# A linear attention with a ReGLU FFN on one core: the first batch in smaller pieces, wo in three loads, the second batch's x turned by DMA, and a new order

## Chip, core and metric

One NeuronCore of a Trainium2 chip runs the whole kernel. The metric is the device time of one execution in microseconds (us); lower is better. The engines are TensorE (PE; its weight loads are shown as PEld), VectorE (DVE), ScalarE (ACT), GpSimd (POOL) and SyncE (SP). SP, ACT and POOL also issue DMA transfers, each from a queue of its own, in the order in which its instructions stand.

## What is computed

```python
# q, k, v: (8 batches, 8 heads, 576 tokens, 64), w_phi: (64, 128)
def phi(x):
    proj = np.einsum('bhsd,df->bhsf', x, w_phi)
    proj = proj - np.max(np.abs(proj), axis=-1, keepdims=True)
    return np.concatenate([np.exp(proj), np.exp(-proj)], axis=-1)
q_p, k_p = phi(q), phi(k)
kv = np.einsum('bhsf,bhsd->bhfd', k_p, v)
z = np.sum(k_p, axis=2)
num = np.einsum('bhsf,bhfd->bhsd', q_p, kv)
den = np.einsum('bhsf,bhf->bhs', q_p, z)[..., None] + 1e-06
x = (num / den).transpose(0, 2, 1, 3).reshape(4608, 512)
# the FFN: w_gate and w_val (512, 1536), w_out (1536, 512)
out = (np.maximum(x @ w_gate, 0) * (x @ w_val)) @ w_out   # float32
```

## The kernel before

**Tiling.** The first 512 tokens of a batch are its main part, 4 chunks of 128; the last 64 are its tail, and the tails of two batches make one chunk of 128. The matmuls are in bf16 and add up in PSUM in f32; a `bank` is one of PSUM's 8 banks (128 partitions by 512 f32).

**Attention.** For k, the 64 x 128 projection is multiplied with the turned k (kT; matmuls L312, "rows"), DVE takes the largest absolute value of each token and head (L319), ACT takes both exponents of the projection (L368, kp) and those of the maximum (L379, ek), and POOL multiplies v with ek (L328, vs) and appends the ek themselves (L414). The kv matmuls (L509 for batches 0 and 1, L486 for the others) add kp against vs over the tokens, and ACT or DVE copies the result to SBUF (L422). For q, the same projection is made twice: as columns (L549), from which ACT takes the exponents qp (L567) without a maximum, and as rows (L312) for the maximum (L319), whose exponent is cq (L583). The n matmuls (L597) multiply qp with kv in three groups of heads; DVE joins their two halves, t = second half times cq (L616) and u = first half plus t (L628), takes the reciprocal of the denominator (L635), and POOL or DVE makes x (L642, xu).

**Turning.** The matmuls need k, q and x with their features on the partitions. `TURN = 2`: for batches 0 and 1 k, q and x are turned by TensorE with an identity matrix (L271, four 128 x 128 blocks a bank for x) and copied from PSUM by DVE or ACT (L284, for x L662). From batch 2 on the DMA crossbar turns them, issued by SP (L292 for k and q, L298 for the tails, L650 for x, one issue per chunk).

**FFN.** Group g = 0 to 7 holds the main tokens of batch g, group 8 the tails. For each block of 128 of the 1536 hidden features, four matmuls make val and four gate (L734), ACT or DVE copies val to SBUF (L749), and DVE makes h = max(gate, 0) times val (L756). Then 12 matmuls with wo per chunk (L791, in three atoms of four), a copy (L805) and the store (L772, for the tails L776 on two queues). `FIRST` says in which pieces of tokens and blocks group 0 goes: it starts when two of its four chunks of x are turned. `LAST` splits the output columns of the last chunk into 352 and 160.

**Loads.** q, k and the weights (wv and wg in thirds, L243; wo, L252) are loaded by POOL's queue, which casts them to bf16; v by SP's queue in f32 (L214, L220). The tails go by L236.

**The order.** All this is cut into "atoms", each a function that issues a few instructions. `ORDER`, a string of numbers, says in which order the atoms are issued; a `'` picks the other engine where there are two, and `z3` issues three matmuls on zeros that only keep TensorE busy (L200). As every engine and queue works in its own order, the string sets what each does next. The sequence of the groups is that of a pipeline: while the FFN of one batch runs on TensorE, the attention of the next batches stands between its matmuls.

## Time and profile before

| | |
|---|---|
| time, median of 3 runs (lowest to highest) | 379.01 us (378.92 to 380.15) |
| profiled execution: span from first to last instruction | 377.4 us |
| difference between the median and this span | 1.6 us |
| mean granted TensorE clock in the profiled execution | 0.995 |
| TensorE busy in the span | 368.1 us |

The profile shows one execution. Busy times count an engine's instructions; "issue ... landing" is the time from a DMA's issue to the arrival of its data; rows of the timeline give the start, the duration, the engine, the line and the tiles, with neighbouring instructions of one kind joined (x4), and in brackets the idle time before them with what ended it. The duration of a joined row of matmuls contains the tail of the last one in the pipeline, so the next row starts before its end.

### The profile page before, as it was taken

The numbers are of one execution on the slowest core, as the hardware profiler recorded it, in microseconds if no ns is written. First come the engines' busy times: TensorE is split into PE (matmuls) and PEld (weight loads), VectorE is DVE, ScalarE is ACT, GpSimd is POOL, SyncE is SP. The second block draws the span as 40 slices with busy tenths as digits, with TensorE's granted clock in tenths as the row PEclk, the third lists the DMA queues.
The fourth block names the chain that finished last, engine by engine and source line by source line (L and its number), as shares of the span: only waits on it lengthen the run. The fifth ranks groups of instructions, "written<-read, shape, count | busy, mean of one in ns | idle before, by whom it ended". The sixth has DMA issues, their size and how long they took to land.

```text
span 377.4 us, 8960 instructions
## 1 busy us (share of the span) xinstructions
PE 368.1 (98%) x3502; PEld 197.4 (52%) x3502; DVE 290.7 (77%) x633; ACT 213.1 (56%) x509; POOL 151.3 (40%) x201
## 2 busy tenths in 40 slices
PE   7789999999999999999999999999999999999996
PEld 4568465546545555464554554465455444444443
DVE  6998999988876799888868886988768927824641
ACT  6997888877687556876765359882740302111101
POOL 5883672488275275901842126933700210000000
PEclk9899999999999999999999999999999999999999
DMA  8999999999489959781289678620410130021004
GB/s 260 205 200 215 233 131 174 219 172 137 89 213 236 165 67 171 144 182 28 59 160 179 96 174 132 130 16 16 128 41 2 29 113 29 2 67 58 2 2 109
DMA packets 87929, 45.10 MB, mean 120 GB/s; under 512 B 55824, under 2 KB 82000, under 8 KB 87888
## 3 DMA queue, kind: packets, MB, share of 16 engines
q1 hardware_dynamic: 60208, 30.42, 37.3%
q0 software_dynamic: 27200, 13.57, 28.8%
q8 instruction: 27, 0.44, 0.5%
q10 hardware_dynamic: 480, 0.56, 0.5%
q14 instruction: 14, 0.11, 0.1%
HBM read 37.78 MB, written 9.44 MB: 125 GB/s over the span
## 4 chain that ended last, share of the span: by engine, by line
PE 92%; ACT 3%; DMA 3%; issue 0%; SPq 0%; DVE 0%; POOL 0%; DVEq 0%
PE pa L734 49%; PE pa L791 25%; PE pa L597 5%; PE pa L312 5%; PE pa L486 4%; PE pa L549 2%; DMA qn<-in_q_dram 2%; ACT qp L567 2%; PE pa L271 1%; PE pa L509 1%; DMA vn<-in_k_dram 1%; ACT kp L368 1%; ACT kv L422 0%; ACT val_sb L749 0%; ACT xT L662 0%
## 5 line engine op out<-in xcount | busy, mean ns | idle before, releaser
L791 PE MATMUL pa<-wo_sb,h 128*128 128x512 bf16 (+2 forms) x444 | 99.9, 373 | 0.0
L734 PE MATMUL pa<-xT,wv_sb 128*128 128x512 bf16 (+1 forms) x400 | 99.3, 370 | 0.1
L734 PE MATMUL pa<-xT,wg_sb 128*128 128x512 bf16 (+1 forms) x400 | 99.3, 370 | 0.0
L756 DVE SCALAR_TENSOR_TENSOR h<-pa,val_sb 128x512 bf16<-128x512 f32 (+1 forms) x112 | 74.6, 669 | 27.2 <-PE pa L734 20.5
L749 ACT CAST val_sb<-pa 128x512 bf16<-128x512 f32 (+1 forms) x67 | 38.1, 575 | 97.1 <-PE pa L734 88.0
L567 ACT ACTIVATE qp<-pa 128x512 bf16<-128x512 f32 x144 | 76.2, 618 | 15.1 <-PE pa L549 14.8
L368 ACT ACTIVATE kp<-pa 128x512 bf16<-128x512 f32 (+1 forms) x152 | 77.4, 605 | 11.1 <-PE pa L312 9.8
L328 POOL TENSOR_TENSOR vs<-vn,ek 128x512 bf16<-128x512 f32 (+1 forms) x68 | 67.4, 1005 | 31.1 <-DMA vn<-in_v_dram 15.2
L734 PEld LDWEIGHTS <-wv_sb 128*128 128x128 bf16 x448 | 41.9, 98 | 44.9 <-issue 1.2
L734 PEld LDWEIGHTS <-wg_sb 128*128 128x128 bf16 x448 | 41.6, 98 | 43.5 <-issue 0.7
L791 PEld LDWEIGHTS <-h 128*128 128x128 bf16 x444 | 40.8, 98 | 44.6 <-issue 0.8
L319 DVE TENSOR_REDUCE mq<-pa 128x4 f32<-128x512 f32 x72 | 46.5, 683 | 10.4 <-PE pa L312 10.1
L319 DVE TENSOR_REDUCE mk<-pa 128x4 f32<-128x512 f32 (+1 forms) x76 | 47.8, 653 | 3.9 <-ACT kp L368 2.3
L642 POOL TENSOR_TENSOR xu<-u,r 128x512 bf16<-128x512 f32 x22 | 22.8, 1041 | 67.4 <-DVE r L635 53.5
L642 POOL TENSOR_TENSOR tT<-u,r 128x512 bf16<-128x512 f32 x14 | 14.6, 1042 | 73.0 <-DVE r L635 41.0
L628 DVE TENSOR_TENSOR u<-pa,t 128x195 f32<-128x195 f32 (+3 forms) x120 | 38.2, 333 | 3.3
L616 DVE TENSOR_TENSOR t<-pa,cq 128x195 f32<-128x195 f32 (+3 forms) x120 | 36.8, 325 | 2.2 <-PE pa L597 1.0
L597 PEld LDWEIGHTS <-qp 128*128 128x128 bf16 x640 | 28.1, 98 | 14.0 <-ACT qp L567 0.9
L749 DVE CAST val_sb<-pa 128x512 bf16<-128x512 f32 (+1 forms) x45 | 30.7, 682 | 4.5 <-PE pa L734 3.0
L597 PE MATMUL pa<-kv,qp 128*128 128x65 bf16 x640 | 31.0, 193 | 0.9 <-ACT qp L567 0.5
L805 DVE COPY out_sb<-pa 128x512 f32<-128x512 f32 x13 | 8.9, 688 | 13.8 <-PE pa L791 13.6
L486 PEld LDWEIGHTS <-kp 128*128 128x128 bf16 x480 | 16.6, 98 | 3.9 <-issue 0.7
(71 smaller groups left out, 278.4 us busy)
## 6 DMA issues: line engine op xcount, KB each, us to landing
vn<-in_v_dram SPq DMA_DIRECT2D x6, 1024.0 KB, 7.3
qn<-in_q_dram POOLq DMA_DIRECT2D x8, 512.0 KB, 8.6
out_dram<-tT SPq DMA_DIRECT2D x16, 256.0 KB, 2.9
out_dram<-out_sb SPq DMA_DIRECT2D x16, 256.0 KB, 2.9
kn<-in_k_dram POOLq DMA_DIRECT2D x6, 512.0 KB, 9.1
wv_sb<-in_moe_w_val_dram POOLq DMA_DIRECT2D x3, 512.0 KB, 10.2
wg_sb<-in_moe_w_gate_dram POOLq DMA_DIRECT2D x3, 512.0 KB, 9.1
wo_sb<-in_moe_w_out_dram POOLq DMA_DIRECT2D x1, 1536.0 KB, 19.5
```

Of the source, the lines that this page charges most:

```text
L319: nc.vector.tensor_reduce(m, some.rearrange("p (c f) -> p c f", f=F), axis=AX.X, op=ALU.max, apply_absolute_value=True,)
L328: eng.tensor_tensor(dst[:, :, s, 0:D], src, ek[:, :, s : s + 1].to_broadcast(list(src.shape)), op=ALU.mult,)
L368: nc.scalar.activation(st["kp"][:, s, 0 : n // 2, par, :], st["banks"][par][:, 0 : n // 2 * F].rearrange("p (a f) -> p a f", f=F), AF.Exp, ...
L567: nc.scalar.activation(x["qp"][:, s, slot].rearrange("p a b -> p (a b)"), st["cols", i][par], AF.Exp, scale=sign,)
L597: nc.tensor.matmul(pn[:, E * (2 * i + s) : E * (2 * i + s + 1)], lhsT=x["qp"][:, s, slot, blk, :], rhs=kv_of(b, lo + i)[:, s, :],)
L616: nc.vector.tensor_tensor(x["t", j][rows, 0:n], ab[:, :, 1], c[:, :, None].to_broadcast([np_, n, E]), op=ALU.mult,)
L628: nc.vector.tensor_tensor(x["u"][rows, lo : lo + n], ab[:, :, 0], x["t", j][rows, 0:n], op=ALU.add)
L642: copy_of(alt, nc.gpsimd, nc.vector).tensor_tensor(x["xu"], x["u"][:, :, 0:D], x["r"].to_broadcast([P, H, D]), op=ALU.mult)
L734: nc.tensor.matmul(ps, lhsT=w[:, dc, P * fi : P * fi + P], rhs=xTs[g][:, dc, lo:hi], start=(dc == 0), stop=(dc == NDC - 1),)
L749: copy_by(copy_of(alt, "ACT", "DVE"))(st["val", n], ps)
L756: nc.vector.scalar_tensor_tensor(st["h2"][:, fi, lo:hi], ps, 0.0, st["val", n], op0=ALU.max, op1=ALU.mult)
L791: nc.tensor.matmul(po, lhsT=st["h2"][:, fi, P * t : P * t + P], rhs=wo_sb[:, fi, c0:c1], start=(fi == 0), stop=(fi == NFC - 1),)
```

## The change

- `FIRST` has five pieces: blocks 0 to 3 with chunk 0 alone, then with chunk 1, blocks 4 to 7 with chunks 0 and 1, blocks 0 to 7 with chunks 2 and 3, blocks 8 to 11 with all. A bank now holds as many blocks side by side as fill 512 columns (four, two or one), so val's copy and h's product always have 512 columns. Group 0 has 12 steps instead of 16.
- `SPLIT`: the column and row matmuls of batch 0's q are issued one bank at a time, and cq is made for each chunk apart.
- `KV_LAST`: the kv matmuls of batch 0 are issued in two parts, the last four blocks of tokens in the second.
- `X_TURN = 1`: x of batch 1 is turned by the DMA crossbar, issued by SP; k and q of batch 1 are still turned on TensorE.
- wo is loaded in three parts of four blocks each.
- The buffer of an xu and of an output tile is chosen by the chunk's number, not by a running count.
- `ORDER` is new. It issues 5 matmuls on zeros instead of 6. (`PLAIN` is empty, so what hangs on it does nothing.)

```diff
+Q_TURN = 2
+X_TURN = 1
-FIRST = ((0, 2, 0, 4), (2, 4, 0, 4), (0, 4, 4, 12))
+FIRST = ((0, 1, 0, 4), (1, 2, 0, 4), (0, 2, 4, 8), (2, 4, 0, 8), (0, 4, 8, 12))
...
-ORDER = """7 z3 82 92 93 83' 84 87 94 86 8 0 98 102 85 89 90 91 88 103 z1 104 96 97 108 105 95 107 106 z1 112
...
+PLAIN = set()
+SPLIT = {(0, 0), (0, 1)}
+KV_LAST = {0: 4}
+ORDER = """z3 84 94 85 86 87 104 95 96 88 89 105 z1 106 114 90 99 9 10 98 97 124 107 109 115 91 116 0 125 134
...
+    def load_wo(i):
+        part = slice(4 * i, 4 * (i + 1))
+        nc.gpsimd.dma_start(
+            out=wo_sb[:, part], in_=moe_w_out.rearrange("(c p) n -> p c n", p=P)[:, part]
         )
+    for i in range(NFC // 4):
+        atoms.add("ld", f"wo{i}")(lambda alt, i=i: load_wo(i))
...
+        last = [x for x in order if x[2] >= 2 * CP * (part + 1) - KV_LAST.get(b, 0)]
+        order = [x for x in order if x not in last] + last
+        cuts = [0, len(order) - len(last), len(order)]
+        for piece, (lo, hi) in enumerate(zip(cuts, cuts[1:])):
...
+            for pars in ((0,), (1,)) if split else ((0, 1),):
+                at = (i, *pars) if split else (i,)
+                @atoms.add("qc", *key, *at)
+                def _(alt, i=i, pars=pars):
+                    for par in pars:
+                        st["cols", i, par] = bank()
...
-            b >= TURN,
-            blocks if b < TURN else None,
+            b >= X_TURN,
+            blocks if b < Q_TURN else None,
...
-        steps = [(fi, 0, SF) for fi in range(NFC)]
+        steps = [(fi, 1, 0, SF) for fi in range(NFC)]
         if g == 0:
-            steps = [(fi, P * lo, P * hi) for lo, hi, f0, f1 in FIRST for fi in range(f0, f1)]
+            steps = [
+                (fi, C // (hi - lo), P * lo, P * hi)
+                for lo, hi, f0, f1 in FIRST
+                for fi in range(f0, f1, C // (hi - lo))
+            ]
+        def half_step(fi, nf, w, lo, hi):
+            ps = bank().rearrange("p (f n) -> p f n", f=nf)
+            for i in range(nf):
+                for dc in range(NDC):
+                    nc.tensor.matmul(
+                        ps[:, i],
+                        lhsT=w[:, dc, P * (fi + i) : P * (fi + i + 1)],
+                        rhs=xTs[g][:, dc, lo:hi],
```

Three places of the new order. First POOL, near the start: here batch 0's v is multiplied (vs), and the loads of wg, wv and of batch 1's q are issued. Before:

```order
L328 TENSOR_TENSOR vs<-vn_109,ek 128x8x64
L414 CAST vs<-ek 128x16
L243 DMA wg_sb<-in_moe_w_gate_dram 128x4x512
L328 TENSOR_TENSOR vs<-vn_109,ek 128x8x64 x2
L414 CAST vs<-ek 128x16
L214 DMA qn<-in_q_dram 128x8x256
L243 DMA wv_sb<-in_moe_w_val_dram 128x4x512
```

And of the change:

```order
L230 DMA qn<-in_q_dram 128x8x256
L349 TENSOR_TENSOR vs<-vn_109,ek 128x8x64 x2
L468 CAST vs<-ek 128x16
L349 TENSOR_TENSOR vs<-vn_109,ek 128x4x64
L468 CAST vs<-ek 128x8
L349 TENSOR_TENSOR vs<-vn_109,ek 128x4x64
L259 DMA wg_sb<-in_moe_w_gate_dram 128x4x512
L259 DMA wv_sb<-in_moe_w_val_dram 128x4x512
```

The load of wg's first third stood between two vs of batch 0 and ahead of batch 1's q; now it stands behind the last vs of batch 0 and behind that q.

Second SP, where batches 1 and 2 meet: qT0 is the turn of batch 2's q, kmT that of the k tails, vn0 the load of batch 2's v, xT_1543 the turned x of batch 1. Before:

```order
L298 DMA_TRANSPOSE kmT_1283<-km_1280 128x4x128
L292 DMA_TRANSPOSE qT0_1390<-qn_1388 128x16x128
L772 DMA out_0_dram<-tT8_1484 128x512
L772 DMA out_0_dram<-out_sb_1596 128x512
L292 DMA_TRANSPOSE kT1_1607<-kn_1503 128x16x128
L214 DMA vn0_1635<-in_v_dram 128x8x256
```

And of the change:

```order
L319 DMA_TRANSPOSE kmT_1508<-km_898 128x4x128
L719 DMA_TRANSPOSE xT_1543<-tT4_1538 128x4x128
L848 DMA out_0_dram<-tT8_1566 128x512
L313 DMA_TRANSPOSE qT0_1634<-qn_1524 128x16x128
L719 DMA_TRANSPOSE xT_1543<-xu_1651 128x4x128
L719 DMA_TRANSPOSE xT_1543<-xu_1672 128x4x128
L719 DMA_TRANSPOSE xT_1543<-tT4_1644 128x4x128
L848 DMA out_0_dram<-tT8_1708 128x512
L230 DMA vn0_1752<-in_v_dram 128x8x256
```

Four turns of x are new on this queue, three of them between the turn of batch 2's q and the load of its v.

Third DVE, its last instructions of the program (tT and out_sb are output tiles, u the buffer of the second piece of the last chunk). Before:

```order
L756 SCALAR_TENSOR_TENSOR h_6191<-pa,val_sb 128x512
L805 COPY tT_6354<-pa 128x512
L805 COPY tT_6388<-pa 128x512
L805 COPY u<-pa 128x160
```

And of the change:

```order
L830 SCALAR_TENSOR_TENSOR h_6237<-pa,val_sb 128x512 x3
L881 COPY tT_6404<-pa 128x512
L881 COPY tT_6412<-pa 128x512
L881 COPY out_sb<-pa 128x512
L881 COPY out_sb<-pa 128x352
```

The piece of 160 columns is copied earlier and by ACT now; the piece of 352 columns comes last and is copied by DVE.

More of the change, by code (lines that the diff above doesn't have):

```diff
@@ L284, in turned_copy @@
         copy_by(by)(st["T"].rearrange("p a b -> p (a b)"), st["pt"][:, 0 : n * P])
-    for b in range(TURN, B):
-        for n in "kq":
+    for b in range(min(TURN, Q_TURN), B):
+        for n, first in (("k", TURN), ("q", Q_TURN)):
+            if b < first:
+                continue
             @atoms.add("turn", n, b)
@@ L310, in rows_of @@
         for j in range(T.shape[1]):
-            for par in range(2):
+            for par in banks:
                 nc.tensor.matmul(
@@ L351, in _ @@
                 st["T"] = T()
-            st["banks"] = [bank(), bank()]
+            st["banks"] = {par: bank() for par in range(2)}
             rows_of(st["T"], st["banks"])
@@ L373, in _ @@
                     )
+        if plain:
+            return
         @atoms.add("kk", *key)
@@ L751, in _ @@
+        for n, (fi, nf, lo, hi) in enumerate(steps):
+            @atoms.add("fv", g, n)
+            def _(alt, n=n, fi=fi, nf=nf, lo=lo, hi=hi):
+                ps = half_step(fi, nf, wv_sb, lo, hi)
+                st["val", n] = sb_g.tile([P, SF], BF16, name="val_sb")
+                copy_by(copy_of(alt, "ACT", "DVE"))(
+                    st["val", n], ps.rearrange("p f n -> p (f n)")
+                )
             @atoms.add("fg", g, n)
-            def _(alt, n=n, fi=fi, lo=lo, hi=hi):
+            def _(alt, n=n, fi=fi, nf=nf, lo=lo, hi=hi):
```

247 lines of the change are left out of this document (130 added, 117 removed), and 45 rows, old and new, of the table ORDER.

## The prediction

> **What bounds the kernel now.** I read the busy times first, then the chain of work that ended last by engine, then what TensorE waits for, then the windows by stage.
>
> ```profile
> PE 368.1 (98%) x3502; PEld 197.4 (52%) x3502; DVE 290.7 (77%) x633; ACT 213.1 (56%) x509; POOL 151.3 (40%) x201
> ...
> PE 92%; ACT 3%; DMA 3%; issue 0%; SPq 0%; DVE 0%; POOL 0%; DVEq 0%
> ```
>
> TensorE is busy for 98% of the 377.4 us span, and 92% of the chain that ended last is TensorE's own work. Its waits, and the windows (columns: stretch; us; PE, PEld, DVE, ACT and POOL busy; granted clock; DMA share; GB/s), say where the rest lies.
>
> ```profile
> PE pa L312 <- DVE tT L284: 1.1, 3, 0.5
> PE pa L200 <- DVE zeros L824: 1.0, 1, 1.0
> ```
>
> ```profile
> 10.00:20.00 10.00, 7.98 (x151) 5.57 (x151) 9.64 (x19) 9.52 (x31) 8.70 (x14) 0.83 1.28 205
> 20.00:30.00 10.00, 9.04 (x198) 7.14 (x197) 9.87 (x35) 9.57 (x22) 8.91 (x12) 1.00 1.40 201
> 30.00:40.00 10.00, 9.84 (x109) 7.40 (x107) 8.48 (x20) 7.86 (x24) 2.06 (x2) 1.00 1.23 239
> 60.00:377.00 317.00, 313.73 (x2729) 162.46 (x2728) 238.09 (x515) 163.74 (x380) 113.44 (x141) 1.00 0.56 103
> ```
>
> From 10 to 30 us DVE and ACT are busy for 95 to 99% and TensorE idles for 2.02 + 0.96 us: the exponents, maxima and divisions of batch 0 set that stage. From 30 us on TensorE idles only 0.16 us in ten, and the same view of the waits, asked from 40 us on, lists none. So two things can move the time: the idle time of TensorE in the first 40 us, and a new wait put into a stretch that now has none.
>
> The chain gives the marks.
>
> ```profile
> 23.46 2.06 ACT qp L567 x4
> 25.62 0.98 ACT qp L567 x2
> ...
> 29.07 1.31 PE pa L734 x12
> ...
> 56.78 0.86 PE pa L791 x4
> ...
> 72.18 2.59 PE pa L734 x12
> ...
> 342.62 20.72 PE pa L734 x96
> ```
>
> The first FFN matmul stands on the chain at 29.07 us, behind batch 0's exponents on ACT; the first matmul with wo at 56.78 us. Late in the kernel 96 matmuls of 512 columns take 20.72 us, so one costs 0.216 us.
>
> **Change, part 1: the start.** In the order of the program, ahead of the first FFN matmul there now stand 9 groups of n matmuls instead of 12, 2 xu instead of 4, and one turned chunk of x instead of two, because FIRST begins with 128 tokens instead of 256.
>
> ```profile
> L616 DVE TENSOR_TENSOR t<-pa,cq 128x195 f32<-128x195 f32 x64 | 21.5, 346 | 1.6 <-PE pa L597 0.8 <-ACT cq L583 0.5
> ```
>
> ```profile
> 68.59 0.39 PE L271 MATMUL pa<-ident,xu 128*128 128x128 bf16 x4
> ...
> 68.81 0.38 PE L597 MATMUL pa<-kv,qp 128*128 128x65 bf16 x7
> ```
>
> That takes 9 of the 24 t and u additions at about 0.3 us each off DVE (2.6 us at most), against which stand one more maximum and copies moved onto DVE: I count DVE's work ahead of that matmul as 1.4 to 2.2 us less, ACT's as 1.9 us less, TensorE's as 1.0 us less. The engines that bind there are DVE and ACT, so the FFN begins 1.4 to 1.9 us earlier. As 1.0 us of TensorE's work ahead only moved behind, the saving in idle time is 0.4 to 0.9 us; I take 0.6. Beside it real work leaves TensorE: the 16 transposes of batch 1's x. Four of them start at 68.59 us and the next kind at 68.81 us, so four cost 0.22 us and sixteen 0.88 us, in a stretch where TensorE never idles. Part 1 and the transposes together: **-1.5 us**. Bounds: -0.5 if the earlier start is eaten again before the first wo matmul, ahead of which ACT has 4 us more work than before (ACT is only 79% busy from 30 to 40 us, so this is mostly hidden); -2.8 if the idle 3.1 us from 10 to 40 us go down by 1.9.
>
> **Part 2: the loads on POOL's queue.** The load of wg's first third is moved behind all of batch 0's vs and the load of q1, and wo is cut in three.
>
> ```profile
> 12.14 0.81 POOL L243 DMA_DIRECT2D wg_sb<-in_moe_w_gate_dram  x1
> ...
> 20.68 0.62 POOL L328 TENSOR_TENSOR vs<-vn,ek 128x256 bf16<-128x256 f32 x1
> ```
>
> ```profile
> wg_sb<-in_moe_w_gate_dram POOLq DMA_DIRECT2D x3, 512.0 KB, 9.1
> ```
>
> It is issued at 12.14 us now; behind the last vs (here 20.68 us, then without one weight load ahead of it, about 19.5 us) and with the median 9.1 us to landing it comes at about 28.6 us. The first gate matmul stands eight matmuls of 128 columns (0.055 us each by the row of four above) behind the first val matmul and wants it at 28.0 (29.07 - 1.5 + 0.4). The gap of 0.6 us can be filled with the rows and n matmuls that stand between; I take 0 and keep the rest for a rival.
>
> ```profile
> 40.95 0.61 POOL L328 TENSOR_TENSOR vs<-vn,ek 128x256 bf16<-128x256 f32 x1 [8.47 <-DMA vn<-in_v_dram]
> ```
>
> The three loads of wo are issued between batch 1's vs, where the one stood ahead of them. POOL waits 8.5 us for v of batch 1 here; on SP that load now stands ahead of the turn of the q tails instead of behind it, so these vs come some us earlier, and the three loads with them, before the first wo matmul: 0, and up to 2 us if v comes as late as now. That batch 0's q matmuls go out one bank at a time, and kv in two pieces, changes no instruction's length: 0, contained in part 1.
>
> **Part 3: batch 1's x by DMA, and less cover for every turned x.** A batch's FFN starts when its last chunk of x has been turned. Between the batch's last n matmul and that point TensorE needs other work: the cover. In the order it is, before and after: batch 2 10.7 and 7.7 us, 3 9.7 and 9.4, 4 13.0 and 10.4, 5 14.5 and 14.8, 6 9.4 and 8.5, 7 11.7 and 6.9, and 8.7 us for batch 1. Batch 7 and 4 are the tight ones.
>
> ```profile
> 298.11 0.54 PE L597 MATMUL pa<-kv,qp 128*128 128x65 bf16 x12
> ...
> 300.86 9.67 PE L791 MATMUL pa<-wo_sb,h 128*128 128x512 bf16 x44
> ...
> 300.96 0.19 DVE L635 RECIPROCAL r<-u 128x8 f32<-128x8 f32 x1
> 301.07 0.64 DVE L319 TENSOR_REDUCE mq<-pa 128x4 f32<-128x512 f32 x1
> ...
> 302.29 1.04 POOL L642 TENSOR_TENSOR xu<-u,r 128x512 bf16<-128x512 f32 x1
> ...
> 304.63 1.22 SPq L650 DMA_TRANSPOSE xT<-xu  x1
> ...
> 310.37 0.81 PE L734 MATMUL pa<-xT,wv_sb 128*128 128x512 bf16 x3
> ```
>
> ```profile
> xT<-xu SPq DMA_TRANSPOSE x1, 2.5
> ```
>
> Batch 7 before: n ends at 298.5, the last xu on POOL at 303.3, the turn is issued at 304.63 behind another and lands 2.5 us later at 307.1; the FFN at 310.37 waits for nothing, with 3.2 us to spare. The need was 8.6 us, and 8.6 against a cover of 6.9 would be a stall of 1.7 us. But in the new order only one group of 6 n matmuls comes that late (12 before), one of the four xu goes from POOL to DVE, and what DVE has between is t and u (0.7), two maxima (1.3) and a reciprocal (0.2); with POOL's 1.04, SP's 1.2 and the rest of the landing (1.3), plus 0.5 us of backlog on DVE (a gate product, the xu and two reciprocals, 2.1 us, against 1.6 us of TensorE's work since) and 0.6 us behind an earlier turn on SP, that is 6.8 us. So I take 0.1 for batch 7, between 0 and 1.7.
>
> ```profile
> 183.06 0.29 PE L597 MATMUL pa<-kv,qp 128*128 128x65 bf16 x4
> ...
> 188.00 1.19 SPq L650 DMA_TRANSPOSE xT<-tT  x1
> ...
> 197.02 1.02 PE L734 MATMUL pa<-xT,wv_sb 128*128 128x512 bf16 x4
> ```
>
> ```profile
> xT<-tT SPq DMA_TRANSPOSE x1, 6.6
> ```
>
> Batch 4 before: n ends at 183.2, the last turn is issued at 188.00 and takes 6.6 us beside a load; it lands at 194.6 with 2.4 us to spare. The cover falls by 2.6: 0.2 us of stall, and up to 1.2 if the turn, now directly behind a load of v on SP's queue, comes a us later. The other batches keep over 1 us: 0.
>
> ```profile
> L650 SPq DMA_TRANSPOSE xT<-xu x12: 1189/1191/1774, 98.5 to 304.6; - x12
> ...
> DMA to landing us min/median/max: 2.4/2.7/6.8
> ```
>
> ```profile
> 58.96 5.21 SPq L292 DMA_TRANSPOSE qT<-qn  x1
> ```
>
> Batch 1's x is new on this path: three of its turns stand on SP behind the turn of q of batch 2, which holds SP until 64.2 us here. Then come three issues of 1.2 us and a landing of 2.7 - 1.2 us behind the last: 69.3, against an FFN of batch 1 that starts at 70.7 (72.18, the chain's next FFN piece, would be 1.5 earlier). I take 0.2, as q of batch 2 is loaded behind wo now; by the worst landing (6.8) the stall is 2.7.
>
> For these 128x128 turns the Trainium skill, "VectorE: DVE Perf Modes", section "Rules for kernel authors", speaks against the change: TensorE where the result may go to PSUM, else the DMA crossbar. By that rule batch 1's x stays on TensorE: the sum would be 0.88 us longer and without the risk just named. The rows, 0.22 us of a busy TensorE against 2.7 us that others hide, favour the crossbar as long as the cover holds.
>
> The loads of v for batch 2 stand behind those turns on SP; its kv matmuls may come late: +0.2 us, between 0 and 1.5. Part 3 together: 0.1 + 0.2 + 0.2 + 0.2 = **+0.7 us** (0 to 7).
>
> **Part 4: the end.** The last piece of the last chunk is now the one of 352 columns on DVE, where it was the one of 160.
>
> ```profile
> 373.84 0.32 DVE L805 COPY u<-pa 128x160 f32<-128x160 f32 x1 [2.00 <-PE pa L791]
> ```
>
> ```profile
> out_dram<-out_sb ACTq DMA_DIRECT2D x1, 88.0 KB, 2.4
> ...
> out_dram<-u ACTq DMA_DIRECT2D x1, 40.0 KB, 2.1
> ```
>
> Behind the last matmul stand a copy and a store. A copy of 512 columns by DVE is 688 ns in the page's groups (L805), so 352 come to about 0.52 us by interpolation, 0.2 more; the store takes 2.4 instead of 2.1 us: **+0.5 us** (0.4 to 0.6).
>
> ```profile
> L805 DVE COPY out_sb<-pa 128x512 f32<-128x512 f32 x13 | 8.9, 688 | 13.8 <-PE pa L791 13.6
> ```
>
> **Sum.** 377.4 - 1.5 + 0 + 0.7 + 0.5 = 377.1 us of span. The median of the runs, 379.01, is 1.6 us above the span of the profiled execution; that lies around it and stays. 377.1 + 1.6 = **378.7 us**, 0.3 less than before. Its own range goes from 377.4 (start -2.8) to 380.5 (start -0.5, v late by 1.0).
>
> **Rivals.** *The covers hold and the start brings its upper bound*: no stall, start -2.5: 377.4 - 2.5 + 0.5 + 1.6 = 377.0 us (376.0 to 377.7). For it: TensorE idles 3.1 us from 10 to 40 us, and smaller first pieces aim at just that. The Trainium skill, "Advanced Engine Details and Errata", section "X-Bar Transpose (TRN2)", says that transposing DMAs are as fast as regular ones; by it no turn would be late. The trace agrees in the median (2.7 us for a turn of 128 KB) but not at the worst (6.8). Against: ACT's 4 us more ahead of the first wo matmul.
>
> *Slower: x lands late.* If a turn needs about a us more than before in its place, the cover no longer holds: batch 7 at its old need 1.7, batch 4 1.2, batch 1 1.0, in all 3.9 instead of the 0.5 counted: 378.7 + 3.4 = 382.1 us (380.2 to 384). It decides at a need above 6.9 us in batch 7 and 10.4 in batch 4, and for batch 1 at a q turn that leaves SP after 65.6 us. For it: before, every cover was at least 2.4 us longer than its need; now two are level. Against: the late work was shifted to earlier places too.
>
> *The start brings nothing*: the late wg, with the second thirds of wv and wg behind it (each about 2.6 us later than its forerunner), holds the FFN at its old time; the transposes are still saved, and ACT's excess costs 0.7 us: 378.7 + 0.6 + 0.7 = 380.0 us (379 to 381.5).
>
> **How the numbers follow.** Forecast 0.40, better start 0.22, x late 0.24, no gain at the start 0.14. A measurement of this kernel can tell 0.3%, 1.1 us, from no change: faster is below 377.9, slower above 380.15. Of the forecast 0.10 is faster, 0.27 within and 0.03 slower; the better start is faster; of the start without gain 0.08 is within and 0.06 slower; x late is slower. Faster 0.32, same 0.35, slower 0.33. The range leaves out 0.1 on each side: 376.4 to 382.4.
>
> **What would show it.** In the profile of the changed kernel: part 1 by the first FFN matmul on the chain, at 27.2 to 27.7 us, and the first wo matmul near 56; part 2 by a wait of TensorE for wg (none above 1 us); part 3 by waits for xT from 60 us on (none for batches 2, 3, 5, 6; under 0.5 us for 1, 4 and 7); the end by 0.5 us more from the last matmul to the end. The forecast is wrong if TensorE waits over 1.5 us in all from 60 us on, or if the FFN starts after 28.5 us.

## The result and the profile after

The changed kernel takes 405.45 us (median of 4 runs, 404.88 to 406.83) against 379.58 us for the kernel before in the same comparison (378.92 to 381.06): ratio 1.0687, 95% interval 1.0654 to 1.072. It is **26 us slower**; the forecast was 378.7, and no rival went beyond 384. The span of the profiled execution is 403.3 us, 25.9 more.

The busy times and the chain's shares of the changed kernel's page:

```profile
PE 372.8 (92%) x3499; PEld 200.9 (50%) x3549; DVE 285.3 (71%) x624; ACT 220.1 (55%) x526; POOL 140.9 (35%) x188
...
PE 62%; ACT 11%; issue 10%; DVE 9%; DMA 4%; SPq 2%; POOL 1%; POOLq 0%; ACTq 0%; DVEq 0%
```

No engine took TensorE's place: DVE, ACT and POOL have lower shares or nearly the same. TensorE is simply idle for 30.5 us where it was idle for 9.3, and some of its matmuls ran slower (busy 372.8 against 368.1 us, for less work). A little of the idle time is not real: this trace holds 3499 matmuls against 3549 weight loads, so about 50 records of matmuls are lacking. The same stretch as in the prediction, from 40 us to the end, in the windows; first the kernel before, then the changed one:

```profile
40.00:377.00 337.00, 333.73 (x3013) 173.35 (x3011) 256.25 (x550) 179.45 (x419) 126.54 (x160) 1.00 0.61 107
```

```profile
10.00:20.00 10.00, 7.69 (x143) 5.19 (x142) 8.36 (x16) 8.07 (x26) 7.65 (x12) 1.00 1.23 247
...
40.00:403.00 363.00, 340.64 (x3013) 178.22 (x3060) 254.49 (x549) 189.48 (x447) 114.86 (x145) 0.99 0.57 102
```

From 40 us on TensorE's idle time went from 3.3 us, all of it behind its last matmul, to 22.4 us, of which about 3.9 lie behind the last matmul and about 3 are places where a record is lacking. (That both windows show 3013 matmuls is chance: their weight loads are 3011 and 3060.) What it waited for there (columns: us in all, times, longest), where the kernel before has no such line:

```profile
PE pa L806 <- DMA xT<-xu: 7.3, 2, 6.2
PE pa L667 <- DVE mk L340: 1.4, 2, 1.2
PE pa L572 <- issue: 1.1, 1, 1.1
```

One wait stands out, and many small ones follow it. To see where the time went I took the time of a mark less the work that TensorE had done until then (each matmul at its pitch), a lag, in both traces:

| mark | lag before, us | lag after, us | grown since the mark above |
|---|---|---|---|
| first FFN matmul (28.9; 29.2 us) | 15.5 | 16.7 | +1.2 |
| first matmul with wo (56.6; 62.2) | 17.0 | 21.6 | +3.4 |
| FFN of batch 1 (72.0; 79.35) | 17.8 | 25.2 | +2.8 |
| wo of batch 3 (about 190 us in the changed kernel) | 21.9 | 32.9 | +3.6 |
| FFN of batch 4 gets going (197.0; 216.7) | 22.7 | 42.8 | +9.1 |
| wo of batch 4 | 23.1 | 46.6 | +3.4 |
| end | 25.7 | 52.2 | +3.0 |

The work itself fell by 1.0 us (347.9 to 346.8). The largest single step is at batch 4. The timeline of the changed kernel there: the last n matmuls of the batch, the last x (xu) on POOL, SP, POOL's load and TensorE.

```profile
198.36 0.29 PE L667 MATMUL pa<-kv,qp 128*128 128x65 bf16 x4 [1.21 <-DVE mk L340]
...
203.46 2.04 POOL L711 TENSOR_TENSOR xu<-u,r 128x512 bf16<-128x512 f32 x2
204.49 1.21 SPq L848 DMA_DIRECT2D out_dram<-out_sb  x2
205.75 0.43 SPq L230 DMA_DIRECT2D vn<-in_v_dram  x1
206.24 1.37 SPq L719 DMA_TRANSPOSE xT<-tT  x1
206.59 0.95 POOL L230 DMA_DIRECT2D kn<-in_k_dram  x1
207.71 3.17 SPq L719 DMA_TRANSPOSE xT<-xu  x2
...
216.67 0.61 PE L806 MATMUL pa<-xT,wv_sb 128*128 128x512 bf16 x1 [6.24 <-DMA xT<-xu]
...
217.50 4.34 PE L806 MATMUL pa<-xT,wv_sb 128*128 128x512 bf16 x10 [0.22 <-issue]
```

And the DMAs issued from 205.7 to 210 us, with their time to landing:

```profile
vn<-in_v_dram SPq DMA_DIRECT2D x1, 1024.0 KB, 6.3
kn<-in_k_dram POOLq DMA_DIRECT2D x1, 512.0 KB, 9.8
...
xT<-xu SPq DMA_TRANSPOSE x2, 7.4
xT<-tT SPq DMA_TRANSPOSE x1, 6.9
```

The three turns are issued beside a load of v (1 MB) and one of k (512 KB) and need 6.9 to 7.8 us each (a view gives the median of its group). The last of them was made ready by POOL at 205.5 us, but SP, with two stores, the load of v and the other two turns ahead of it, issued it only at 209.64. TensorE, with nothing else to do, waits 6.24 us. Then its clock is halved. A window behind the restart (the last three columns: granted clock, DMA share, GB/s):

```profile
218.00:219.00 1.00, 1.00 (x4) 0.38 (x3) 0.00 (x0) 0.40 (x1) 0.00 (x0) 0.50 1.92 88
```

The clock is back at 1.00 from 222 us on. Twelve matmuls (one record is lacking) take 5.0 us, from 216.67 to 221.68, which at 0.216 us each would be 2.6: the halved clock costs 2.4 us on top of the wait. The mark of the table is the first of these matmuls, so the wait makes 6.2 of the 9.1 us of its step, small waits from 191 to 210 us make the rest, and the 2.4 us of the clock belong to the step below it.

The end, in the timeline: the last copy, which was one of 160 columns and 0.32 us.

```profile
399.10 0.53 DVE L881 COPY out_sb<-pa 128x352 f32<-128x352 f32 x1 [1.10 <-PE pa L867]
```

### The profile page after: what moved, and what is told of

It reads as the page before. It is cut to its first block, busy times and chain, and to the rows that moved or that the text cites. A ratio compares the mean times of both kernels' runs of the same rounds, so it can differ in the third digit from the quotient of the medians.

```text
span 403.3 us, 8963 instructions
## 1 busy us (share of the span) xinstructions
PE 372.8 (92%) x3499; PEld 200.9 (50%) x3549; DVE 285.3 (71%) x624; ACT 220.1 (55%) x526; POOL 140.9 (35%) x188
## 4 chain that ended last, share of the span: by engine, by line
PE 62%; ACT 11%; issue 10%; DVE 9%; DMA 4%; SPq 2%; POOL 1%; POOLq 0%; ACTq 0%; DVEq 0%
PE pa L806 37%; PE pa L867 14%; ACT kp L407 5%; PE pa L667 3%; PE pa L333 3%; ACT qp L633 3%; DVE mk L340 2%; DMA xT<-xu 2%; PE pa L540 2%; DVE u L698 2%; DVE t L686 2%; DMA vn<-in_k_dram 2%; PE pa L614 2%; SPq L719 1%; PE pa L572 1%
## 5 line engine op out<-in xcount | busy, mean ns | idle before, releaser
L806 PE MATMUL pa<-xT,wv_sb 128*128 128x512 bf16 (+2 forms) x413 | 95.4, 361 | 10.6 <-DMA xT<-xu 7.3
L830 DVE SCALAR_TENSOR_TENSOR h<-pa,val_sb 128x512 bf16<-128x512 f32 x108 | 73.8, 688 | 39.1 <-PE pa L806 34.5
L806 PE MATMUL pa<-xT,wg_sb 128*128 128x512 bf16 (+2 forms) x420 | 93.1, 355 | 0.7
L821 ACT CAST val_sb<-pa 128x512 bf16<-128x512 f32 x71 | 41.7, 595 | 89.3 <-PE pa L806 65.9
L349 POOL TENSOR_TENSOR vs<-vn,ek 128x512 bf16<-128x512 f32 (+1 forms) x65 | 64.6, 1006 | 42.8 <-ACT ek L421 32.5
L806 PEld LDWEIGHTS <-wv_sb 128*128 128x128 bf16 x480 | 43.8, 99 | 54.1 <-DMA xT<-xu 7.4
L711 POOL TENSOR_TENSOR xu<-u,r 128x512 bf16<-128x512 f32 x18 | 18.6, 1040 | 79.2 <-DVE r L705 72.2
L821 DVE CAST val_sb<-pa 128x512 bf16<-128x512 f32 x37 | 25.3, 689 | 13.4 <-PE pa L806 13.1
L711 POOL TENSOR_TENSOR tT<-u,r 128x512 bf16<-128x512 f32 x10 | 10.4, 1041 | 62.6 <-DVE r L705 62.3
L881 ACT COPY tT<-pa 128x512 f32<-128x512 f32 x13 | 7.6, 588 | 30.7 <-PE pa L867 30.7
```

The source lines that it names most:

```text
L349: eng.tensor_tensor(dst[:, :, s, 0:D], src, ek[:, :, s : s + 1].to_broadcast(list(src.shape)), op=ALU.mult,)
L711: copy_of(alt, nc.gpsimd, nc.vector).tensor_tensor(x["xu"], x["u"][:, :, 0:D], x["r"].to_broadcast([P, H, D]), op=ALU.mult)
L806: nc.tensor.matmul(ps[:, i], lhsT=w[:, dc, P * (fi + i) : P * (fi + i + 1)], rhs=xTs[g][:, dc, lo:hi], start=(dc == 0), stop=(dc == NDC - 1),)
L821: copy_by(copy_of(alt, "ACT", "DVE"))(st["val", n], ps.rearrange("p f n -> p (f n)"))
L830: nc.vector.scalar_tensor_tensor(st["h2"][:, fi : fi + nf, lo:hi], ps, 0.0, st["val", n].rearrange("p (f n) -> p f n", f=nf), op0=ALU.max, ...
```

## The experiments

The theories at the outset: **late turns** (a turn of x issued beside a load lands with the load, and the new order puts turns there), against **the parts** (the smaller pieces, the kv cut and the three loads of wo cost something themselves) and **the start** (what is lost is lost in batch 0 and only carried on). The letters in an expectation are explained in that expectation. In the diffs the atoms of `ORDER` have names: `xd.b.c` issues the turn of chunk c of batch b, `xu` makes x, `ld` loads, `fv` and `fo` are matmuls of the FFN with wv and wo (`fo` with its copy and store), `km` is a maximum of k's projection on DVE, `ke` its exponents on ACT. All medians of the kernel before in these comparisons lie between 379.45 and 380.5 us.

### Which half of the order

*h_before_then_after*: the order of before up to the FFN of batch 1, then the order of the change.

```diff
-ORDER = <order of before>
+ORDER = <order of before up to the first fv.1> + <order of the change, what is left of it>
```

> The kernel before with its own start (old FIRST, x of batch 1 turned on TensorE, one load of wo) up to the first FFN matmul of batch 1; from there on the atoms that are left stand in the order of the change. Theory A: the waits behind batch 1 come back without the new start, 379.0 + 19 = 398 us, 392 to 400. Rival B (they are an echo of the start): 378 to 383 us.

Measured: 403.95 us (403.09 to 405.24), ratio 1.0608 (1.0545 to 1.0671), above the expected range (392 to 400). Nearly the whole loss is there without the start of the change. What TensorE waits for:

```profile
PE pa L734 <- DMA xT<-tT: 8.9, 1, 8.9
PE pa L734 <- DMA xT<-xu: 2.3, 1, 2.3
```

The first is batch 4, the second batch 7, the two that the prediction called tight, with waits beyond the bounds it gave (1.2 and 1.7 us).

*h_after_then_before*: the reverse, the change's order and parts up to the first FFN matmul of batch 1, then the order of before.

```diff
-ORDER = <order of the change>
+ORDER = <order of the change up to the first fv.1> + <order of before, what is left of it>
```

> The changed kernel (all its parts: FIRST, SPLIT, KV_LAST, X_TURN = 1, three loads of wo) in its own order up to the first FFN matmul of batch 1; from there on the atoms that are left stand in the order of the kernel before. The trace of the changed kernel has lost 7.4 us against the one before at that point, counted as time less TensorE's own work, and 19.1 us more behind it. Theory A (the order behind batch 1 is the larger loss, the start the smaller): about 379.0 + 7.4 - 1.0 (less work for TensorE) = 385.5 us, 384 to 388. Rival B (the start brings late everything that follows, and the later waits are only its echo): 398 to 406 us, as the late state is kept. Rival C (the start does not lose by itself): 377 to 380 us.

Measured: 394.15 us (393.59 to 395.65), ratio 1.0354 (1.0292 to 1.0416), between the expected ranges. By the first wo matmul of batch 1 the lag is 34.4 us against 19.0 before, and it grows no further against it. The two halves do not add up to the whole: 14 and 23 us against 26. In this kernel TensorE stands twice for nearly 3 us where the orders are joined and before, and each time its clock is halved afterwards:

```profile
PE pa L806 <- DVE mk L340: 2.9, 1, 2.9
PE pa L572 <- issue: 2.8, 1, 2.8
```

The view puts the first to DVE, whose maximum was done at 83.3 us; by the times, what TensorE still waited for then was the last turn of batch 1's x, issued at 75.87 us, 1.6 us behind a load of k, and landed at 83.98. (In the change itself that turn landed at 79.26 us and TensorE waited 0.57 us.) So the halves show that both contain losses, not how large each is in the change.

### The parts or the order

*parts_old_order*: every part of the change, in the order of before, the pieces put where the old FFN steps stood.

```diff
-ORDER = <order of the change>
+ORDER = <order of before, each old step of group 0 replaced by the new pieces>
```

> All parts of the change (the new FIRST, SPLIT, KV_LAST, X_TURN = 1, wo in three loads, buffers by index) in the order of the kernel before, atom for atom, where an atom was cut its pieces side by side, and batch 1's turns on SP as in the run with x of batch 1 alone, each behind its xu. Theory A (the new order is the whole loss, the parts cost nothing): 377 to 381 us. Rival (the smaller pieces or the cut loads themselves cost): 384 us or more.

Measured: 395.15 us (394.04 to 396.79), ratio 1.04 (1.0341 to 1.0459). That is in the range of the rival, by which the parts themselves cost something (384 us or more), but the trace says otherwise:

```profile
PE pa L540 <- POOL vsm L437: 5.9, 1, 5.9
```

This wait and one of 2.1 us at L572 are for v of batch 1 and 2: at the old steps' places the new pieces do twice the work early and push batch 1's attention back, and the load of the v tails had come to stand late on SP. The placement was mine, so it says nothing of the parts.

*parts_same_place*: again all parts but the turned x of batch 1 (`X_TURN = 2`), each new step now where the same work was finished before, the split atoms side by side.

```diff
-X_TURN = 1
+X_TURN = 2
-ORDER = <order of the change>
+ORDER = <order of before: split atoms side by side, new steps where their work ended>
```

> All parts of the change but x of batch 1, which TensorE turns as before (the new FIRST, SPLIT, KV_LAST, wo in three loads, buffers by index), in the order of the kernel before; each new FFN step of the first group stands where the old steps of the same amount of work ended, so that the two chunks' steps stay where they were. Theory A (the parts by themselves cost nothing, and by themselves bring nothing): 378 to 381.5 us. Rival (pieces of 128 columns, cut loads or buffers by index cost by themselves): 384 us or more.

Measured: 380.42 us (10 runs, 379.75 to 383.94), ratio 1.0023 (0.9987 to 1.006): no difference. The smaller pieces, the kv cut and the three wo loads cost and bring nothing that can be measured. **The loss is in the order**, which decides beside what each step runs, together with the turned x of batch 1, which this kernel leaves out.

### The turned x of batch 1 alone

*b_x1*: the kernel before, with x of batch 1 turned by the crossbar at the places where TensorE turned it.

```diff
-            b >= TURN,
+            b >= 1,
 ...
-xT.1.c xc.1.c
+xd.1.c
```

> The kernel before with one part of the change alone: x of batch 1 is turned by the DMA crossbar on SP, at the places where TensorE turned it. TensorE loses 16 transposes, 0.9 us. The last turn is issued near 69.3 us and lands 2.7 us later (6.8 at worst), the FFN of batch 1 starts at 72.0. Theory A (this part costs little, the order is what costs): 378 to 381 us. Rival (x of batch 1 on the crossbar is itself what makes the change slow, with loads beside it): over 383 us.

Measured: 395.68 us (394.92 to 397.5), ratio 1.0395 (1.033 to 1.0459), in the slower theory's range. The wait, and what SP issued last before it ended:

```profile
PE pa L734 <- DMA xT<-xu: 14.0, 1, 14.0
```

```profile
75.38 4.01 SPq L236 DMA_DIRECT2D vm<-in_v_dram  x2
79.48 3.28 SPq L650 DMA_TRANSPOSE xT<-tT  x1
...
84.18 1.26 SPq L650 DMA_TRANSPOSE xT<-xu  x1
```

The four turns were issued at 70.84, 73.48, 79.48 and 84.18 us and took 6.8, 10.2, 6.0 and 2.5 us; a load of batch 2's v stands on SP at 72.15. The last of them landed at 86.69 us and ended the wait. It landed fast but was issued late: SP had been held for 4.0 us by the loads of the v tails and for 3.3 us by the third turn. So this wait is one for the place on SP and for the landings together. With 0.88 us of transposes taken off TensorE the kernel is 15 us slower.

*b_x1s*: the same, but the turns right behind the division that makes x, ahead of that v, its tails and a turn of k.

```diff
-turn.k.3 ld.v2 ld.vm1 ... xd.1.0 xd.1.1 xd.1.2 xd.1.3
+xd.1.0 xd.1.1 xd.1.2 xd.1.3 turn.k.3 ld.v2 ld.vm1
```

> As the run with x of batch 1 alone on the crossbar, but on SP each turn stands directly behind the making of its xu, and the loads of v and of the v tails for batches 2 and 3 and the turn of k of batch 3 stand behind all four. In the first such run the load of v (1 MB) stood ahead of three of the turns and these landed 6 to 10 us after their issue; TensorE waited 14 us. Theory A (a turn is late only where a load stands ahead of it on SP): the last xu is ready near 69 us, lands near 71.5, TensorE waits 0 to 1 us and saves 0.9: 377.5 to 380 us. Rival (the crossbar itself is slow in this stretch, POOL's loads being in flight as well): 383 us or more.

Measured: 390.46 us (389.09 to 391.8), ratio 1.0273 (1.0214 to 1.0332). The theory that only the place on SP counts fell: 9.7 us of wait are left. The turns and the loads in the timeline, and what the DMAs issued from 69.5 to 72 us took:

```profile
69.64 0.92 POOL L214 DMA_DIRECT2D qn<-in_q_dram  x1
70.16 1.31 SPq L650 DMA_TRANSPOSE xT<-xu  x1
71.56 1.61 SPq L650 DMA_TRANSPOSE xT<-tT  x1
...
81.16 1.86 PE L734 MATMUL pa<-xT,wv_sb 128*128 128x512 bf16 x4 [9.71 <-DMA xT<-xu]
```

```profile
qn<-in_q_dram POOLq DMA_DIRECT2D x1, 512.0 KB, 11.1
out_dram<-out_sb SPq DMA_DIRECT2D x1, 256.0 KB, 4.3
...
xT<-xu SPq DMA_TRANSPOSE x1, 10.0
xT<-tT SPq DMA_TRANSPOSE x1, 9.4
```

The load of q on POOL's queue, another queue, was issued 0.5 us ahead of the third turn. It landed at 69.64 + 11.1 = 80.7 us; the two turns behind it at 80.2 and 81.0. The two turns issued before that load took 4.2 to 4.3 us.

*b_x1t*: as b_x1s, with that load (and those of the q tails) moved behind the first FFN matmuls of batch 1, and a store behind the turns.

```diff
-ld.qm1 ld.q3 turn.qm.1 ... fv.1.0
+fv.1.0 ld.qm1 ld.q3 turn.qm.1
-fo.0.1.0.2 ... xd.1.2
+xd.1.2 fo.0.1.0.2
```

> As the second run with x of batch 1 alone on the crossbar (390.5 us); in it the last two turns were issued at 70.2 and 71.6 us, 0.5 and 1.9 us behind the load of q of batch 3 on POOL's queue (69.6, landed at 80.7), and landed with it at 80.2 and 81.0. Here that load and the q tails are issued behind the start of batch 1's FFN, and on SP a store that held the third turn stands behind the turns. Theory C (a turn that is issued while a load of POOL's queue is in flight lands with that load; with none in flight it takes 2.4 to 2.7 us): all four land within 3 us, TensorE waits 0 to 1.5 us: 378.0 to 381 us. Rival (turns behind stores or behind the turn of q, or batch 1's state itself, are slow): 385 us or more.

Measured: 382.65 us (6 runs, 381.61 to 384.59), ratio 1.0082 (1.0054 to 1.0111), between the two expected ranges. The turns land after 4.6, 3.7, 3.1 and 2.4 us (within 3 was expected), and the wait for x, 14.0 and then 9.7 us, is gone. The longest wait of TensorE from 60 us on, the others being at most 0.4 us:

```profile
PE pa L486 <- POOL vsm L395: 1.4, 1, 1.4
```

The 0.8% that stay come later (the lag grows by 3.3 us between the FFN of batch 1 and its wo, against 1.0 in the kernel before); that the moved loads are missed there would fit, and is not shown. So three kernels that differ nearly only in the order of transfers (b_x1t also has four wo matmuls with their copy and store, and turns of k and q, at other places) lie at +15, +10 and +3 us. From the first to the second the place on SP was mended, from the second to the third the load in flight was taken away: both made x late.

### Batch 4's turns

*a_sp4*: the change, with three turns of batch 4 ahead of two stores and a load of v on SP. Nothing else is moved.

```diff
-fo.3.1.0.2' fo.3.3.0.2 ld.v6 ... xd.4.1 xd.4.2 xd.4.0
+xd.4.1 xd.4.2 xd.4.0 fo.3.1.0.2' fo.3.3.0.2 ld.v6
```

> The changed kernel, only SP's queue differs: the last three turns of batch 4's x stand ahead of two stores and the load of v of batch 6 instead of behind them. In the trace these turns were issued at 206.2 to 209.6 us, the last landed 7 us later at 216.6, TensorE waited 6.4 us for it and then ran at half its pace for 5 us (2.7 us lost). Theory A (SP's queue and the load beside the turns make batch 4's x late): the turns go out 2 to 4 us earlier and land without the load; 4 to 9 us less, 396.5 to 401.5 us. Rival (the turns wait for POOL and the landing is slow anyway, or the time returns in the next wait): 0 to 2 us less, 403.5 to 405.5 us.

Measured: 399.77 us (397.85 to 399.93), ratio 1.0481 (1.0404 to 1.0558), 5.7 us less than the change, in the range 396.5 to 401.5. Timeline, and DMAs issued from 205 to 210.5 us:

```profile
207.97 2.79 SPq L719 DMA_TRANSPOSE xT<-xu  x2
210.03 0.94 POOL L230 DMA_DIRECT2D kn<-in_k_dram  x1
```

```profile
kn<-in_k_dram POOLq DMA_DIRECT2D x1, 512.0 KB, 8.8
xT<-xu SPq DMA_TRANSPOSE x2, 2.5
```

The last turn goes out half a us ahead of the load of k and takes 2.4 us; the wait of batch 4 is gone, and the halved clock with it.

*a_sp_all*: the change, every turn of x right behind the division that makes it.

```diff
-xu.b.c ... xd.b.c
+xu.b.c xd.b.c
```

> The changed kernel; on SP each turn of x of batches 1 to 7 stands directly behind the making of its xu, so ahead of the stores and loads that stood between. Theory A (places on SP make x late in batches 4, 7, 2 and 1): the 5.7 us of batch 4 that the run with batch 4 alone gained, 1.3 to 2 in batch 7, about 1 in batch 2, up to 1 in batch 1: 396 to 399 us. Rival (the stores that now stand behind hold the output buffers, and TensorE waits for their banks instead): 400 us or more.

Measured: 404.1 us (401.48 to 406.05), ratio 1.0628 (1.0554 to 1.0701): hardly anything is gained, and the general rule "turn as early as you can" fell. The time lies in the rival's range (400 us or more), though not by the rival's cause. Timeline, and the DMAs issued from 209 us on:

```profile
209.13 0.94 POOL L230 DMA_DIRECT2D kn<-in_k_dram  x1
209.91 1.22 SPq L719 DMA_TRANSPOSE xT<-xu  x1
...
217.24 5.28 PE L806 MATMUL pa<-xT,wv_sb 128*128 128x512 bf16 x12 [4.25 <-DMA xT<-xu]
```

```profile
kn<-in_k_dram POOLq DMA_DIRECT2D x1, 512.0 KB, 7.7
...
xT<-xu SPq DMA_TRANSPOSE x1, 7.2
```

Here the load went out 0.8 us ahead of the last turn, which landed with it, at 217.1 us. In a_sp4 and in a_sp_all that turn leaves SP within half a us of the same time. Which of the two comes first decides over 4.7 us of landing, a wait of 4.2 us and again a halved clock.

### What else is in the 26 us

*a_wo_early*: the change, the three loads of wo at 31 us instead of 47 to 53 us.

```diff
-ld.wv2 ... ld.wo0 ... ld.wo1 ... ld.wo2
+ld.wv2 ld.wo0 ld.wo1 ld.wo2
```

> The changed kernel with its three loads of wo issued directly behind the last weight load (near 31 us) instead of between batch 1's vs (47.5 to 52.5 us). In the traces of the change and of two other runs with this start TensorE stands 1.3 to 3.0 us inside batch 1's kv matmuls at 53 to 56 us with no engine or data named, while these loads keep the DMA engines full; in the kernel before the same matmuls run through. Theory A (the stand is TensorE's own code, fetched behind the loads): it goes, 1 to 4 us less, 401.5 to 404.5 us. Rival (it is not tied to these loads, or the loads of k and of the tails, now behind wo, come too late): 405 to 409 us.

Measured: 403.55, 410.95, 411.4 and 635.2 us. The runs differ too much, and nothing is concluded from them.

*a_fix2*: the change with four moves of transfers alone: batch 4's turns as in a_sp4, two turns of batch 7 ahead of a store, the load of batch 3's k behind the start of batch 1's FFN, and wo at 31 us.

```diff
+xd.4.1 xd.4.2 xd.4.0 fo.3.1.0.2' fo.3.3.0.2 ld.v6
+xu.7.1.0 xd.7.2 xd.7.3
+fv.1.0 ld.k3
+ld.wv2 ld.wo0 ld.wo1 ld.wo2
```

> The changed kernel with four moves of transfers and nothing else: batch 4's turns ahead of the stores and the load of v (as in the run that gained 5.7 us), batch 7's second and third turn ahead of a store, the load of k of batch 3 behind the start of batch 1's FFN, and the three loads of wo at 31 us. Theory C (transfers' places are most of the loss): 399.8 - 1.3 (batch 7) - 0.7 (batch 1) - 2.5 (the stand inside batch 1's kv matmuls and the half clock behind it) = 395.3 us, 393.5 to 397; about 16 us stay for the order of the compute atoms and for the start. Rival (other waits take their place): 399 us or more.

Measured: 396.75 us (395.57 to 400.88), ratio 1.0475 (1.0405 to 1.0544); expected 393.5 to 397. TensorE's longest waits from 40 us on:

```profile
PE pa L667 <- DVE mk L340: 1.4, 2, 1.2
```

The waits for x are down to 0.2 us. The stand of 1.1 us in the kv matmuls (L572) is gone too, though TensorE's instructions are the same; what the traces show of this stand is told in the last section. What is left is many waits for DVE. What DVE itself waits for, in a_fix2:

```profile
DVE mk L340 <- ACT kp L407: 15.3, 13, 2.2
```

The maximum (mk) needs nothing from ACT: both read the same projection in the same PSUM bank, and whichever is issued later waits until the other has read. The same line in the kernel before and in the change:

```profile
DVE mk L319 <- ACT kp L368: 2.3, 5, 1.1
```

```profile
DVE mk L340 <- ACT kp L407: 24.1, 14, 9.9
```

The longest wait of the change, 9.9 us, only follows from TensorE's wait at batch 4; without it 14.2 us are left, and a_sp4, where that wait is gone, has 15.5 us in 14. The order did not put more maxima behind exponents: in both orders 31 of the 76 maxima of k stand behind the exponents of their bank. They are in part other ones (18 are the same), and it is the wait there that grew.

*a_mk*: a_fix2 with 13 maxima ahead of the exponents that read the same bank.

```diff
-ke.b.i.j km.b.i.j
+km.b.i.j ke.b.i.j
```

> The run with the four moves of transfers (396.8 us), and on DVE 13 maxima of k moved ahead of the two exponents of ACT that read the same bank, where they stood behind them. In that run DVE stood 15.3 us in these 13 places until ACT had done its exponents (2.3 us in 5 places in the kernel before), and TensorE waited 4.9 us in all for DVE's maxima and additions. Theory D (these stands of DVE hold up the release of banks and the making of x, and so TensorE): DVE's wait for these exponents falls below 4 us and 4 to 8 us of the time go, 388.5 to 393 us. Rival (ACT then waits for DVE in the same places, and the order is simply tight everywhere): 394.5 us or more.

Measured: 392.8 us (391.82 to 396.62), ratio 1.0337 (1.0287 to 1.0387); expected 388.5 to 393. The same line now:

```profile
DVE mk L340 <- ACT kp L407: 3.1, 3, 1.4
```

By the medians the swap is worth about 4 us, though the runs of the two kernels touch (391.8 to 396.6 and 395.6 to 400.9 us) and ACT waits more, as the rival had it (14.3 us for such maxima, 10.2 before). The trace is of this kernel's slowest run and can't show the 4 us as a difference of spans; from the FFN of batch 1 on its lag grows by 13.0 us, against 16.1 in a_fix2.

## Why the prediction was wrong

**The step that failed is part 3**, the place of the turned x. It gave batch 4 a stall of 0.2 us, "up to 1.2 if the turn, now directly behind a load of v on SP's queue, comes a us later". Measured: batch 4 waits 6.24 us and loses another 2.4 by the halved clock. Four things were wrong in it:

- *The way from the last n matmul to the last turn was taken over from the trace of before.* Before, it was 11.4 us for batch 4: the last x was ready 4.8 us after the last n matmul and its turn issued at once, and the turn took 6.6 us. The prediction kept all of this and added at most a us. In the change it is 18.1 us: x is ready after 7.0 us, 2.2 more; its turn then stands 4.1 us on SP behind two stores, a load of v and two other turns; and it takes 7.0 us, 0.4 more. So the prediction had the slow landing of batch 4 in its sum; what it had wrong is above all SP's queue, and then when x is made. The order of the change could be read for the stores and the load. a_sp4, which moves the turns ahead of them, gains 5.7 us: there the last x was ready only at 208.94 us, its turn was issued at 209.54, ahead of the load of k, and took 2.4 us.
- *The loads on the other queue were not asked for.* The prediction took 6.6 us for batch 4 because the trace had it, but did not ask for each turn which load stands before it on *any* queue. The trace of before had the reason to ask: that turn was issued at 188.00 us, 0.1 us behind a load of k on POOL's queue. For batch 1 this did no harm in the change: its turns took up to 6.6 us beside a load of k, and TensorE waited 0.57 us, where the prediction had 0.2 with 2.7 at the worst. In the order of before the same x makes TensorE wait 14.0 us (b_x1).
- *A wait was priced at its own length.* Behind batch 4's wait the clock is at 0.50 for some us. The Trainium skill, "TensorE: Matmul & The Clock Gate", Part 1, has the clock halved after an idle window of about 3.4 us and restored after as long a busy one; the traces agree in the halving and about in the time it lasts (3.2 to 5.9 us from the end of the wait), but here shorter waits were enough in some cases: 1.9 us in a_sp4, 2.1 in parts_old_order.
- *A turn that stands behind a store.* Batch 7 was allowed 0.1 us. In the timeline of the change its last three turns follow a store on SP:

```profile
328.34 0.33 SPq L848 DMA_DIRECT2D out_dram<-out_sb  x1
328.76 1.22 SPq L719 DMA_TRANSPOSE xT<-xu  x1
...
331.39 1.22 SPq L719 DMA_TRANSPOSE xT<-xu  x1
...
333.97 1.02 PE L806 MATMUL pa<-xT,wv_sb 128*128 128x512 bf16 x4 [1.10 <-DMA xT<-xu]
```

The first two of them had been ready since 325.8 and 327.1 us; SP waited for the copy that the store sends. TensorE stood 1.1 us: within the bound of 1.7 that was kept for it, by another cause.

All this is about 10 of the 26 us: 8.6 at batch 4, 1.1 at batch 7 and 0.6 at batch 1. The rest is in part 1 (below) and in a term that the prediction put at nothing without a reason: what the new order costs in all other stages from 40 us on.

**Part 1** (-1.5 us) failed as well. The first FFN matmul was to come at 27.2 to 27.7 us; it came at 29.21, 0.3 later than the 28.91 us of before in the same view. The work was taken off as counted: TensorE is busy for 22.6 us until then instead of 23.5, and DVE for 8.36 instead of 9.64 us from 10 to 20 us. But the load of k now ends TensorE's waits more often. The waits of TensorE up to 40 us in the change, with the line that grew:

```profile
PE pa L290 <- DMA vn<-in_k_dram: 2.3, 3, 1.0
```

The line of before for the same tile (L271) reads 0.6 us. The prediction had asked what the engines save, not what is late next. The landing of that load varied between the runs from 7.4 to 9.3 us. In h_after_then_before, with the same order up to there, its last part landed at 7.5 us and the first FFN matmul came at 28.48 us: so about 0.7 us go with the load, and even then the 27.2 to 27.7 us were not reached. What holds the rest is not settled. The saved transposes did come: TensorE's work is 1.0 us less, 0.88 were counted.

**Part 2** was right: wg's first third landed at 28.20 us (28.6 forecast), and TensorE never waits for wg. The three loads of wo, priced 0, were issued at 47.5, 51.7 and 52.5 us and landed at 53.3, 57.2 and 61.5, just ahead of their use; the parts alone cost nothing (parts_same_place), and in this order two of them are in flight when TensorE stands at L572, which does not show that they are the cause.

**Part 4** was right: +0.5 forecast, +0.6 measured (copy 0.53 instead of 0.32 us, store 2.3 instead of 2.1).

**The rivals.** "x lands late" had the right mechanism and the wrong size: 382.1 us, worked out from turns that come about one us late, where batch 4's came 6.7 us later after the last n matmul than before. The premise that one tight stage decides was too narrow in another respect: DVE's maxima wait longer behind ACT's exponents, and putting 13 of them ahead is worth about 4 us (a_mk), in a stretch in which the prediction saw only x as a danger. Nothing in it asked whether DVE and ACT still read each bank in a good order. The prediction also held that the crossbar is the better place for batch 1's x as long as the cover holds. In the three kernels that tried this alone, x or something behind it came late, and the time rose by 3 to 15 us for the 0.88 us of TensorE that were saved.

**What is shown and what stays open.** Of the 26 us, moved transfers give back 8.7 (a_fix2), the order of readers about 4 (a_mk). About 12 to 13 us remain: 392.8 us against 379.5 to 380.4. Their place is known in part, some 4 to 5 us up to the first wo matmul and the rest, in the trace of a_fix2, in waits of TensorE of 1.2 us or less, most of them for DVE; which moves of the order cause them was not tried one by one. None of the kernels beats the one before.

## What to carry to other kernels

Before a transfer is moved, list for every late and short one what stands ahead of it on its own queue and when that can go, and which loads are in flight on all queues at its new place; price it by the slow case unless none is. An order in which TensorE never waits has no free places: judge a new one by each producer's distance to its consumer, for transfers and for two engines that read one bank, not by the work it takes away. A wait of TensorE of 2 us or more can cost 1.6 to 3 us more in clock (half of the 3.2 to 5.9 us for which it was halved).

## What the hardware showed

- *A turn by the crossbar beside a load.* The kept traces hold 404 turns of x, 128 KB each (without a_wo_early). Of the 251 with no load in flight none took more than 4.6 us, and 200 took at most 2.7. All 27 that were issued within 1.1 us behind a load of 512 KB or 1 MB, on its own queue or another, took 6.5 to 10.8 us and landed from 2 us before to 2 us after the load (217.1 and 216.8 us in a_sp_all). The others took 2.4 to 10.2 us. At batch 4, 0.5 us ahead of the load or 0.8 us behind it decides (a_sp4, a_sp_all). The Trainium skill, "DMA: Bandwidth & Descriptors", section "Queues, rings and completion order", has each DMA engine alternate between queues packet by packet, by which a turn should not have to stay for a load on another queue that is four times its size; the trace does not agree. Why it stays was not tried.
- *Not every transfer suffers so.* Beside the same q load in b_x1s a store of 256 KB issued in the same stretch landed after 4.3 us, where the turns took 9.4 and 10.0.
- *TensorE stands in the middle of a run of matmuls.* With "issue" as its reason it stood for 1.1 us in the change, 1.9 in a_sp4, 2.6 in a_sp_all, 2.8 in h_after_then_before and 1.1 in parts_same_place, always in the kv matmuls (L572), and not at all in a_fix2, with the same instructions for TensorE. Loads in flight don't explain it alone: in parts_same_place the loads of wo had landed by 51.5 us, and TensorE stood from 54.2 to 55.3. In all five a packet of 16 KB on the DMA queue that the profile calls `instruction` ended 1.3 to 1.6 us before TensorE went on; in a_fix2 one ended about 2 us before TensorE reached that place. That TensorE's instructions came late would fit; the profile does not say for which engine the packet was, so it is argued, not shown.
- *The halved clock.* After 6.2 us of waiting the clock was 0.50 from 214.8, still in the wait, to about 221.6 us; after 2.8 us (h_after_then_before) from 55.6 to 59.0; after 1.9 us (a_sp4) from 55.9 to 59.3. After 1.1 us (batch 7) it was not halved, nor after 1.9 us in a_mk (at 83.2 us) and 2.3 us in h_before_then_after (batch 7). So the length of the wait alone does not decide.
